# Small edits at the start of a two-attention kernel: two weight loads on another DMA queue, a weight split earlier, a DMA group earlier, another rotation of PSUM banks, another operation in the row maxima

## The chip, the cores and the metric

The kernel runs on one core of one Trainium2 chip. The metric is the device time of one execution in microseconds. A profiled execution additionally leaves a trace: its span runs from the first to the last instruction, and its own time is a little longer than its span.

## The reference

The inputs are float32: 2048 rows of 576, and 32 heads of 18 columns for each of two attentions. Attention A has its own keys and values for every head; attention B shares one key and one value head among its 32 query heads. A gate per row mixes the two results.

```python
def _A_ref(x, wqkv, wo):                       # 32 heads, Dh = 18
    q, k, v = (x @ wqkv) split by head
    p = softmax(q @ k^T * Dh ** -0.5)
    return (p @ v) @ wo
def _B_ref(x, wq, wk, wv, wo):                 # k and v shared by 32 heads
    q = (x @ wq) split by head; k = x @ wk; v = x @ wv
    return (softmax(q @ k^T * Dh ** -0.5) @ v) @ wo
g = sigmoid((x * gate_w).sum(-1, keepdims=True))
return g * _A_ref(...) + (1 - g) * _B_ref(...)
```

## The kernel before

**Numbers as pairs.** Every float32 operand is cut into a high part h (rounded to the type that TensorE multiplies at full rate) and a low part l, the difference. ScalarE or another engine writes h, VectorE or GpSimd writes l = value - h. A projection tile is 14 matmuls: h*h and the two mixed products over the four full rows of 128 of the inner dimension (x dimension 0 to 511), and two matmuls for the last 64, stacked.

**Stage 1, projection of tiles 0 to 2.** All weight columns stand in `wall` as 14 tiles of 128 columns. Tiles 0, 1 and 2 are projected first, for the row chunks c = 0 to 3 of 512 rows each: (tile, chunk) = (0,0), (1,0), (2,0), then the list `FIRST` = (0,1), (1,1), (2,1), (0,2), (0,3), (1,2), (2,2), (1,3), (2,3). Tile 0 holds the shared key, the gate column, the shared value and the first queries of B. x arrives transposed by DMA in two half chunks (`xsh`) and three full ones (`xs`), and `chunk(c)` cuts chunk c: for each half `split_x` has ScalarE write h (`xh`, L388) and VectorE write l (`xl`, L394) and the last 64 rows (L398). `chunk(2)` stands before the result of (1,1) is taken, `chunk(3)` before that of (2,1). `leave` takes a finished projection out of PSUM: ScalarE L284, for tile 0 also L287, VectorE L289. It then stores it to DRAM: tile 0's rows for the first heads by SP's queue (`kq`), everything else by Pool's queue (`qk`). For chunks 1 and 3 of tile 0 it also forms the difference of two key chunks: chunk 1's on GpSimd (L305, L240, L242, stored as `kd`), chunk 3's on VectorE and ScalarE (`ke`). `shared_v` transposes the shared value out of tile 0's results (L326).

**DMA queues.** `dma()` (L163) issues from SP's queue unless told otherwise. An engine's queue is in order: a store that waits for its data holds up everything behind it. SP loads nearly everything and stores `kq`, `kd` and `z_d`. After chunk 0 of tile 0 is stored, SP loads x's last chunk (`load_x(4)`), and then the weights of tiles 3 and 4 (`load_w`, tile `wst`), each as one transfer of 128 rows and two of 64. `first_back` loads the rows back that the next stage needs first (`kdb`, `qs`, `ksb`); `rows_back` loads the others.

**Stage 2, the lead.** The weights of tiles 3 and 4 are projected in half steps (letters A and B: matmuls of 64 rows on two halves of the array, L963), interleaved by a string written out by hand with the row maxima of the first heads. An x in that string is a matmul (L1115) that ScalarE takes out (`xd`, L1119), a y one that VectorE takes with a running maximum (`junk`, `mx`, L1125). GpSimd adds and cuts the results of tiles 3 and 4 (L1101, L240, L242). `prep_w` cuts a weight tile (L250 on ScalarE, L251 on VectorE): tile 3's after the seventh entry of `FIRST`, tile 4's inside the lead. `max_rows` closes the maxima of a head: a reduction, a transpose, and the pair h, l of the result (`mh`, L240 and L242). It runs on VectorE for heads 0 and 1 and with GpSimd for the others.

**Stage 3, the main part.** For each of the 64 heads: scores (L740 maxima, L695 scores), the exponential on ScalarE (L748), the maxima on VectorE (L704), and the products with v accumulated in `acc` (L755). Half steps of the remaining projections are woven in by strings written out by hand.

**Banks.** Seven PSUM banks are handed out. In stage 1 `clk.turn` does it: kind "s" takes banks 0 to 2 in turn, for projections, and kind "m" banks 3 to 6, for the transposes of `shared_v`. From stage 2 on `Clock.first` picks the bank that its own estimate frees first; `turn` leaves behind in what order the banks were given out.

Of the kernel before, what the change touches and what calls it, by code (L numbers as in the profile page):

```python
# [8 lines left out]
F32 = mybir.dt.float32  # L9
F32R = mybir.dt.float32r  # L10
BF16 = mybir.dt.bfloat16
AF = mybir.ActivationFunctionType
OP = mybir.AluOpType
# [15 lines left out]
NT = 5  # L29
FIRST = ((0, 1), (1, 1), (2, 1), (0, 2), (0, 3), (1, 2), (2, 2), (1, 3), (2, 3))  # L30
PRODS = (("h", "h"), ("h", "l"), ("l", "h"))
PROJ = [(a, b, k, 128) for a, b in (("h", "h"), ("l", "h"), ("h", "l")) for k in range(NKT - 1)] + \
# [15 lines left out]
class Clock:  # L48


    def __init__(self):
        self.free = [0.0] * 7
        self.t = self.act = self.dve = self.last = 0.0
        self.mode, self.begun, self.tail = "", [0.0, 0.0], [0.0, 0.0]
        self.turns, self.count, self.held, self.diffs, self.copies = {"s": 0, "m": 0}, 0, {}, [], []
        self.cleared, self.half = 0.0, HALF_MM

    def turn(self, which):
        n = self.turns[which]
        self.turns[which] += 1  # L60
        self.count += 1
        k = n % 3 if which == "s" else 3 + n % 4
        self.free[k] = -1e6 + self.count
        return k

# [91 lines left out]
def gated_mix_kernel(ctx: ExitStack, tc: tile.TileContext, xT, wall, wv, wo, out):  # L157
# [3 lines left out]
    def dma(o, i, eng=None):  # L161
        o, i = (x.bitcast(F32) if x.dtype == F32R else x for x in (o, i))
        return (eng or nc.sync).dma_start(o, i)  # L163
# [46 lines left out]
    def in_turn(which):  # L210
        return bank_tile(clk.turn(which))
# [29 lines left out]
        if l is not None:  # L241
            eng_l.tensor_tensor(l, src, h.bitcast(F32), op=OP.subtract)  # L242

    def load5(t, src, rest=None):
        dma(t[:, 0:4, :], src[0:512, :].rearrange("(p k) m -> p k m", p=P))
        dma(t[0:64, 4, :], src[512:576, :], rest)
        dma(t[64:128, 4, :], src[512:576, :], rest)

# [1 line left out]
        nc.scalar.activation(w["h"], st, AF.Copy)  # L250
        eng_l.tensor_tensor(w["l"], st, w["h"].bitcast(F32), op=OP.subtract)  # L251

    def load_w(mt, rest=None):
        st = wpool.tile([P, NKT, P], F32, name="wst", bufs=5)
        load5(st, wall[mt], rest)
        return st

    def prep_w(st):
        w = {y: wpool.tile([P, NKT, P], F32R, name=f"w{y}", bufs=3) for y in "hl"}
        split_w(st, w, nc.vector)  # L260
        return w
# [4 lines left out]
    def project(mt, c, w, parts=1):  # L266


        fp = in_turn("s")
        g = 512 // parts  # L270
        for i in range(parts):
            products(fp, w, c * 512, g * i, g)
        return leave(mt, c, fp)
# [47 lines left out]
        return c, st  # L321

    def shared_v(c, st):
        pv = in_turn("m")
        for j in range(4):
            nc.tensor.transpose(pv[:, 18 * j:18 * j + 18],  # L326
                                st[ROW_VB:ROW_VB + 18, j * P:(j + 1) * P],
                                ident[ROW_VB:ROW_VB + 18, ROW_VB:ROW_VB + 18])
        nc.vector.tensor_copy(vb[:, 4 * c:4 * c + 4, 0:18],
                              pv[:, 0:72].rearrange("p (j d) -> p j d", d=18))  # L330
# [35 lines left out]
    with tc.tile_pool(name="xs", bufs=1, side="right") as xsp:  # L366
        XS = []

        def load_x(c, rest=None):
            half = c < 2  # L370
            XS.append(xsp.tile([P, NKT, 256 if half else 512], F32, name="xsh" if half else "xs", bufs=2 if half else 3))
            load5(XS[c], xT[:, 256 * c:256 * c + 256] if half else xT[:, 512 * (c - 1):512 * c], rest)

        def main_w(st):

            w = {y: wpool.tile([P, NKT, P], F32R, name=f"w{y}", bufs=3) for y in "hl"}
            nc.scalar.activation(w["h"][:, 0:4], st[:, 0:4], AF.Copy)
            nc.vector.tensor_tensor(w["l"][:, 0:4], st[:, 0:4], w["h"][:, 0:4].bitcast(F32), op=OP.subtract)
            return w

        def last_w(st, w):
            nc.scalar.activation(w["h"][:, 4], st[:, 4], AF.Copy)
            nc.vector.tensor_tensor(w["l"][:, 4], st[:, 4], w["h"][:, 4].bitcast(F32), op=OP.subtract)

        def split_x(c):
            xs = XS[c // 2 + 1][:, :, 256 * (c % 2):256 * (c % 2) + 256] if c > 1 else XS[c]
            cs = slice(c * 256, (c + 1) * 256)
            nc.scalar.activation(X["h"][:, :, cs], xs, AF.Copy)  # L388
            low_x(c, xs)
            last_x(c, xs)  # L390

        def low_x(c, xs):
            cs = slice(c * 256, (c + 1) * 256)
            nc.vector.tensor_tensor(X["l"][:, :, cs], xs[:, 0:4], X["h"][:, 0:4, cs].bitcast(F32), op=OP.subtract)  # L394

        def last_x(c, xs):
            xh = X["h"][64:128, 4, c * 256:(c + 1) * 256]
            nc.vector.tensor_tensor(xh, xs[64:128, 4], xh.bitcast(F32), op=OP.subtract)  # L398

        W = [load_w(0, nc.scalar)]  # L400
        load_x(0, nc.scalar)
        nc.scalar.activation(ones, ones, AF.Copy)
        W.append(load_w(1, nc.gpsimd))
        W.append(load_w(2, nc.gpsimd))
        load_x(1, nc.gpsimd)

        warm = in_turn("m")
        for i in range(6):
            nc.tensor.matmul(warm[:, 0:304], ident, vb.rearrange("p k d -> p (k d)"), start=True, stop=True)
        for c in range(2, 4):  # L410
            load_x(c)
        dma(ones_r.rearrange("a (b c) -> (a b) c", c=32), ones)

        x0, xh = XS[0], X["h"][:, :, 0:256]
        ST = [W.pop(0) for _ in range(3)]
        WP = [main_w(ST[0])]
        nc.scalar.activation(xh[:, 0:2], x0[:, 0:2], AF.Copy)
        nc.vector.tensor_copy(xh[:, 2:4], x0[:, 2:4])
        low_x(0, x0)
        WP.append(main_w(ST[1]))  # L420
        WP.append(main_w(ST[2]))
        last_w(ST[0], WP[0])
        nc.scalar.activation(xh[:, 4], x0[:, 4], AF.Copy)
        last_x(0, x0)
        last_w(ST[1], WP[1])
        last_w(ST[2], WP[2])
        split_x(1)
        FP = [in_turn("s") for _ in range(3)]
        for n in ((0, 12), (12, 14)):
            for mt in range(3):  # L430
                products(FP[mt], WP[mt], 0, 0, 256, *n)
        keep = []

        def chunk(c):
            split_x(2 * c)
            split_x(2 * c + 1)

        for mt in range(3):
            if mt == 2:
                chunk(1)  # L440
                shared_v(*keep.pop())
            products(FP[mt], WP[mt], 0, 256, 256)
            keep.append(leave(mt, 0, FP[mt]))
            keep = [k for k in keep if k]
            if mt == 0:
                load_x(4)
                for m in range(3, NT):
                    W.append(load_w(m))
        for n, (mt, c) in enumerate(FIRST):
            if n == 1:  # L450
                chunk(2)
            if n == 2:
                chunk(3)
            if keep and keep[0][0] <= n - 2:
                shared_v(*keep.pop(0)[1])
            done = project(mt, c, WP[mt], 2 if n == 0 else 1)
            if done:
                keep.append((n, done))
            if (mt, c) == (0, 2):
                first_back()  # L460
            if (mt, c) == (0, 3):
                rows_back()
            if n == 6:
                WP.append(prep_w(W.pop(0)))

    xdp = ph1.enter_context(tc.tile_pool(name="xdp", bufs=1, side="right"))
    small = ctx.enter_context(tc.tile_pool(name="small", bufs=1, side="left"))
# [238 lines left out]
    def max_rows(u, eng=nc.gpsimd):  # L706
# [5 lines left out]
        mt = lead.tile([P, 32], F32, name="mt")  # L712
        nc.vector.transpose(mt, m)  # L713
        mh = lead.tile([P, 2, 32], F32R, name="mh")
        split(mt, mh[:, 0, :], mh[:, 1, :], eng, eng)
        md = m_d[u % 4]
        dma(md, mh.rearrange("p a f -> p (a f)"))
        for b in (SB, MB) if u > NU - 3 else (SB,):
# [368 lines left out]

    def lead_units():
        yield
        for mt in range(3, NT):  # L1090
            w = WP.pop()
            for c in range(4):
                if (mt, c) == (3, 1):
                    for _ in range(NT - 4):
                        WP.append(prep_w(W.pop(0)))
                st = stp.tile([P, 512], F32, name="pst", bufs=3)
                st2 = xdp.tile([P, 512], F32, name="pst2", bufs=2)

                def done(mt=mt, c=c, st=st, st2=st2):
                    hl = stp.tile([P, 2, 512], F32R, name="phl", bufs=4)  # L1100
                    nc.gpsimd.tensor_tensor(st, st, st2, op=OP.add)  # L1101
                    split(st, hl[:, 0, :], hl[:, 1, :], nc.gpsimd, nc.gpsimd)
                    dma(qk_d[:, mt * P:(mt + 1) * P, c * 512:(c + 1) * 512].rearrange("a p f -> p a f"), hl,
                        nc.gpsimd)

                yield Unit([(w[a][:, k, :], X[b][:, k, c * 512:(c + 1) * 512]) for a, b, k, _ in PROJ],
                           512, (st, st2), done, how="both", upper=-1)

    def lead_max(what, low):
        M, h = pairs[what].pop(0)  # L1110
# [187 lines left out]
```

## Time and profile before

| | us |
|---|---|
| median of 3 runs | 2635.0 |
| lowest, highest | 2634.32, 2636.1 |
| profiled execution, its own time | 2633.82 |
| its span | 2632.0 |
| stage 1 in the trace | 0 to 50.5 |
| the lead | 50.5 to about 91 |

In the timeline rows the columns are start, duration, engine, line, operation, written tile and read tiles, shapes and count; a bracket holds the time that the engine had been idle and what ended the idle time. Rows marked SPq, and the DMA rows of POOL, are the issue of a transfer, not the transfer. PEld is the weight load of a matmul; it stands in order ahead of its matmul, so a PEld that waits for a PSUM bank holds TensorE up. The queue table counts packets, MB and the time that their packets took as a share of the 16 DMA engines; q1 is the queue that SP feeds, q0 the one that GpSimd feeds.

### The profile page before, as it was taken

The numbers are of one execution on the slowest core, as the hardware profiler recorded it, in microseconds if no ns is written. First come the engines' busy times: TensorE is split into PE (matmuls) and PEld (weight loads), VectorE is DVE, ScalarE is ACT, GpSimd is POOL, SyncE is SP. The second block draws the span as 40 slices with busy tenths as digits, with TensorE's granted clock in tenths as the row PEclk, the third lists the DMA queues.
The fourth block names the chain that finished last, engine by engine and source line by source line (L and its number), as shares of the span: only waits on it lengthen the run. The fifth ranks groups of instructions, "written<-read, shape, count | busy, mean of one in ns | idle before, by whom it ended". The sixth has DMA issues, their size and how long they took to land.

```text
span 2632.0 us, 66889 instructions
## 1 busy us (share of the span) xinstructions
PE 2621.7 (100%) x25213; PEld 1404.5 (53%) x25213; DVE 2395.4 (91%) x4575; ACT 2447.6 (93%) x4862; POOL 850.5 (32%) x1087
## 2 busy tenths in 40 slices
PE   9999999999999999999999999999999999999999
PEld 7655545545455455554554555545555544545665
DVE  6899999999999999999999999999998999999883
ACT  5999999999999999999999999999999999999887
POOL 3611000211364535644554446443310020012113
PEclk9999999999999999999999999999999999999999
DMA  8412112212343234323544344434432332234312
GB/s 259 140 54 62 36 48 59 75 48 74 96 123 105 91 97 120 113 89 93 152 130 137 119 138 141 142 118 121 141 95 76 101 98 85 61 88 126 110 56 92
DMA packets 176328, 270.28 MB, mean 103 GB/s; under 512 B 58905, under 2 KB 137193, under 8 KB 164625
## 3 DMA queue, kind: packets, MB, share of 16 engines
q1 hardware_dynamic: 159813, 212.70, 28.2%
q0 software_dynamic: 15152, 51.79, 5.3%
q8 instruction: 198, 3.24, 0.5%
q10 hardware_dynamic: 1040, 1.52, 0.2%
q14 instruction: 125, 1.02, 0.1%
HBM read 190.26 MB, written 66.90 MB: 98 GB/s over the span
## 4 chain that ended last, share of the span: by engine, by line
PE 98%; DMA 1%; DVE 0%; ACT 0%; SPq 0%; POOL 0%; issue 0%; ACTq 0%; DVEq 0%
PE acc L755 39%; PE bank L695 29%; PE bank L740 17%; PE bank L963 11%; PE bank L278 1%; PE bank L1115 0%; PE bank L943 0%; DMA xsh<-xT 0%; PE acc L767 0%; DMA R<-r_d 0%; SPq L163 0%; POOL oacc L936 0%; DMA wst<-wall 0%; PE bank L1017 0%; DMA sm<-sum_d 0%
## 5 line engine op out<-in xcount | busy, mean ns | idle before, releaser
L748 ACT ACTIVATE pt<-bank 128x512 f32<-128x512 f32 x4096 | 2146.4, 616 | 120.4 <-PE bank L740 68.7
L704 DVE TENSOR_REDUCE mx<-bank 128x1 f32<-128x512 f32 x3002 | 1886.9, 684 | 118.2 <-PE bank L740 60.3
L740 PE MATMUL bank<-qs,ksb 56*128 56x512 f32 x2688 | 906.8, 424 | 0.0
L695 PE MATMUL bank<-ksb,qs 54*128 54x512 f32 x2270 | 806.4, 426 | 0.0
L755 PE MATMUL acc<-pt,vb 128*19 128x256 f32 (+3 forms) x6144 | 553.2, 455 | 0.0
L695 PEld LDWEIGHTS bank<-ksb,qs 54*128 54x128 f32 x2270 | 382.8, 184 | 318.8 <-ACT pt L748 190.3
L755 PE MATMUL acc<-pt,vg 128*19 128x512 f32 (+3 forms) x5952 | 535.0, 455 | 0.0
L740 PEld LDWEIGHTS bank<-qs,ksb 56*128 56x128 f32 x2688 | 441.1, 184 | 153.9 <-DVE mx L704 63.8
L740 PE MATMUL bank<-qs,ksa 56*128 56x512 f32 x1408 | 466.6, 425 | 0.0
L695 PE MATMUL bank<-ksa,qs 54*128 54x512 f32 x1232 | 439.2, 426 | 0.0
L701 DVE CUSTOM_DVE_ANT_0 junk<-bank,xb 128x512 bf16<-128x512 f32 x500 | 342.9, 686 | 29.4 <-PE bank L740 23.6
L698 ACT ACTIVATE xb<-bank 128x512 f32<-128x512 f32 x500 | 292.6, 606 | 13.7 <-PE bank L740 3.2
L695 PEld LDWEIGHTS bank<-ksa,qs 54*128 54x128 f32 x1232 | 207.8, 184 | 151.1 <-ACT pt L748 87.4
L240 POOL CAST mh<-mt 128x32 fp32r<-128x32 f32 x62 | 13.0, 210 | 831.1 <-DVE mt L713 608.8
L740 PEld LDWEIGHTS bank<-qs,ksa 56*128 56x128 f32 x1408 | 225.5, 184 | 84.2 <-DVE mx L704 31.3
L755 PEld LDWEIGHTS acc<-pt,vb 128*19 128x19 f32 x6144 | 123.1, 97 | 203.1 <-issue 169.6
L755 PEld LDWEIGHTS acc<-pt,vg 128*19 128x19 f32 x5952 | 119.7, 97 | 206.2 <-issue 180.2
L240 POOL CAST rhl<-rst 128x292 fp32r<-128x292 f32 (+2 forms) x81 | 34.0, 420 | 486.7 <-issue 316.4
L963 PE MATMUL bank<-xr,wrh 64*128 64x292 f32 (+1 forms) x1134 | 167.9, 300 | 0.0
L695 PE MATMUL bank<-kdb,qs 54*128 54x512 f32 x372 | 159.8, 430 | 0.0
L963 PEld LDWEIGHTS bank<-xr,wrh 64*128 64x128 f32 x1134 | 139.5, 186 | 2.8
L558 POOL TENSOR_TENSOR xr<-xst,xr 128x876 fp32r<-128x876 f32 (+1 forms) x63 | 130.4, 2070 | 0.0
(171 smaller groups left out, 2397.0 us busy)
## 6 DMA issues: line engine op xcount, KB each, us to landing
qs<-qk SPq DMA_DIRECT2D x366, 144.0 KB
xst<-xT SPq DMA_DIRECT2D x54, 438.0 KB
ksa<-qk SPq DMA_DIRECT2D x132, 144.0 KB
qk<-rhl POOLq DMA_DIRECT2D x54, 292.0 KB, 4.3
ksb<-qk SPq DMA_DIRECT2D x60, 144.0 KB
qk<-phl POOLq DMA_DIRECT2D x16, 512.0 KB, 5.4
onh<-oh POOLq DMA_DIRECT2D x32, 256.0 KB, 3.9
onl<-ol POOLq DMA_DIRECT2D x32, 256.0 KB, 4.7
```

What stands on the lines that cost most here:

```text
L240: eng_h.tensor_copy(h, src)
L278: nc.tensor.matmul(fp[:, p0:p0 + g], w[a][:kr, k, :], X[b][:kr, k, x0 + p0:x0 + p0 + g], start=(n == 0), stop=(n == len(PROJ) - 1))
L558: nc.gpsimd.tensor_tensor(x[:, 5:8, 0:n], t0, x[:, 0:3, 0:n].bitcast(F32), op=OP.subtract)
L695: nc.tensor.matmul(pm, qs[u % 3][b:b + 54, i * P:(i + 1) * P], k, start=True, stop=True)
L698: nc.scalar.activation(MX["x", u, i], pm, AF.Relu)
L701: nc.vector.tensor_tensor_reduce(junk, pm, MX.pop(("x", u, i)), 1.0, -3e38, op0=OP.add, op1=OP.max, accum_out=MX[u][:, i, c:c + 1])
L704: nc.vector.tensor_reduce(MX[u][:, i, c:c + 1], pm, axis=AX.X, op=OP.max)
L740: nc.tensor.matmul(ps, kst(u)[b:b + 56, i * P:(i + 1) * P], qs[u % 3][b:b + 56, c * 512:(c + 1) * 512], start=True, stop=True)
L748: nc.scalar.activation(pt, ps, AF.Exp, scale=SCALE)
L755: nc.tensor.matmul(acc[32 * j:32 * j + 19, a:b], v_of(u, i), PT[u, i, j][:, a:b], start=(i == 0), stop=(i == 15), skip_group_check=True)
L963: nc.tensor.matmul(u.fp[op][:, 0:u.n], x[b:b + 64], y[b:b + 64], start=(n == 0), stop=(n == last))
```

## The change

The change has five parts.

1. `load_w` and `load5` get an argument `main`, and both transfers' queues become GpSimd's for tiles 3 and 4; the loop stands where it stood, after chunk 0 of tile 0 was stored.
2. `prep_w` is called after the seventh and after the eighth entry of `FIRST`, so tile 4 is cut there and not in the lead.
3. `first_back` is called after (2,1), one entry of `FIRST` earlier than before.
4. Projections and `shared_v` of stage 1 draw from one rotation "g" of all seven banks; the warm-up matmuls keep "m".
5. Where `max_rows` runs on VectorE, h is written by `tensor_tensor` with the maximum of a value and itself, not by a CAST.

```diff
-        k = n % 3 if which == "s" else 3 + n % 4
+        k = n % 3 if which == "s" else 3 + n % 4 if which == "m" else n % 7
...
-    def load5(t, src, rest=None):
-        dma(t[:, 0:4, :], src[0:512, :].rearrange("(p k) m -> p k m", p=P))
+    def load5(t, src, rest=None, main=None):
+        dma(t[:, 0:4, :], src[0:512, :].rearrange("(p k) m -> p k m", p=P), main)
...
     def project(mt, c, w, parts=1):
-        fp = in_turn("s")
+        fp = in_turn("g")
...
     def shared_v(c, st):
-        pv = in_turn("m")
+        pv = in_turn("g")
...
-        FP = [in_turn("s") for _ in range(3)]
+        FP = [in_turn("g") for _ in range(3)]
...
             if mt == 0:
                 load_x(4)
                 for m in range(3, NT):
-                    W.append(load_w(m))
+                    W.append(load_w(m, nc.gpsimd, nc.gpsimd))
...
-            if (mt, c) == (0, 2):
+            if (mt, c) == (2, 1):
                 first_back()
             if (mt, c) == (0, 3):
                 rows_back()
-            if n == 6:
+            if n in (6, 7):
                 WP.append(prep_w(W.pop(0)))
+        while keep:
+            shared_v(*keep.pop(0)[1])
...
-        split(mt, mh[:, 0, :], mh[:, 1, :], eng, eng)
+        if eng is nc.vector:
+            eng.tensor_tensor(mh[:, 0, :], mt, mt, op=OP.max)
+            eng.tensor_tensor(mh[:, 1, :], mt, mh[:, 0, :].bitcast(F32), op=OP.subtract)
+        else:
+            split(mt, mh[:, 0, :], mh[:, 1, :], eng, eng)
...
     def lead_units():
-                if (mt, c) == (3, 1):
-                    for _ in range(NT - 4):
-                        WP.append(prep_w(W.pop(0)))
```

TensorE's instructions keep their order from the first to the last; only the banks that they name differ. What moves on the other engines is shown in three pieces.

SP's queue in stage 1, as a piece of the difference: `xs` is x's last chunk, `kq`, `kd` and `z_d` are the stores of tile 0, `kdb`, `qs` and `ksb` the loads of `first_back`.

```order
 L163 DMA xs<-xT 64x512 x2
-L163 DMA wst<-wall 128x512
-L163 DMA wst<-wall 64x128 x2
-L163 DMA wst<-wall 128x512
-L163 DMA wst<-wall 64x128 x2
 L163 DMA kq<-phl 54x2x512
```

The six weight transfers (rows with x2 are two) leave the place between x's last chunk and the stores of (0,1).

GpSimd's queue at the same place of the program, as a piece of the difference: `qk<-phl 24x2x512` is the store of (0,0), the two of 128x2x512 are those of (1,0) and (2,0).

```order
 L163 DMA xsh<-xT 64x256 x2
 L163 DMA qk<-phl 24x2x512
+L163 DMA wst<-wall 128x512
+L163 DMA wst<-wall 64x128 x2
+L163 DMA wst<-wall 128x512
+L163 DMA wst<-wall 64x128 x2
 L163 DMA qk<-phl 128x2x512 x2
```

They now stand behind the store of (0,0) and ahead of the stores of (1,0) and (2,0).

ScalarE's end of stage 1 and start of the lead, before: `phl` rows take (2,2), (1,3) and (2,3) out of PSUM, `wh` rows cut a weight tile, `xd` and `pst` rows belong to the lead.

```order
L284 ACTIVATE phl<-bank_525 128x512
L250 ACTIVATE wh<-wst 128x640
L284 ACTIVATE phl<-bank_548 128x512
L284 ACTIVATE phl<-bank_567 128x512
L1119 ACTIVATE xd<-bank_630 128x512
L1119 ACTIVATE xd<-bank_638 128x512
L1119 ACTIVATE xd<-bank_648 128x512
L1119 ACTIVATE xd<-bank_660 128x512
L1119 ACTIVATE xd<-bank_670 128x512
L973 ACTIVATE pst<-bank_617 128x512
L250 ACTIVATE wh<-wst 128x640
```

And with the change:

```order
L284 ACTIVATE phl<-bank_525 128x512
L250 ACTIVATE wh<-wst 128x640
L284 ACTIVATE phl<-bank_548 128x512
L250 ACTIVATE wh<-wst 128x640
L284 ACTIVATE phl<-bank_571 128x512
L1120 ACTIVATE xd<-bank_634 128x512
```

Tile 4's cut goes from behind the first `pst` of the lead to between (1,3) and (2,3); VectorE's L251 moves with it.

More of the change, by code (lines that the diff above doesn't have):

```diff
@@ L54, in __init__ @@
         self.mode, self.begun, self.tail = "", [0.0, 0.0], [0.0, 0.0]
-        self.turns, self.count, self.held, self.diffs, self.copies = {"s": 0, "m": 0}, 0, {}, [], []
+        self.turns, self.count, self.held, self.diffs, self.copies = {"s": 0, "m": 0, "g": 0}, 0, {}, [], []
         self.cleared, self.half = 0.0, HALF_MM
@@ L251, in split_w, with load_w @@
         eng_l.tensor_tensor(w["l"], st, w["h"].bitcast(F32), op=OP.subtract)
-    def load_w(mt, rest=None):
+    def load_w(mt, rest=None, main=None):
         st = wpool.tile([P, NKT, P], F32, name="wst", bufs=5)
-        load5(st, wall[mt], rest)
+        load5(st, wall[mt], rest, main)
         return st
@@ L443, in gated_mix_kernel @@
             keep.append(leave(mt, 0, FP[mt]))
-            keep = [k for k in keep if k]
             if mt == 0:
@@ L447, in gated_mix_kernel @@
                 for m in range(3, NT):
-                    W.append(load_w(m))
+                    W.append(load_w(m, nc.gpsimd, nc.gpsimd))
+            keep = [k for k in keep if k]
         for n, (mt, c) in enumerate(FIRST):
@@ L1089, in lead_units, with done @@
         yield
-        for mt in range(3, NT):
-            w = WP.pop()
-            for c in range(4):
-                if (mt, c) == (3, 1):
-                    for _ in range(NT - 4):
-                        WP.append(prep_w(W.pop(0)))
[L1096 to L1107, printed above, removed]
+        for mt, c in [(mt, c) for mt in range(3, NT) for c in range(4)]:
+            w = WP[mt]
+            st = stp.tile([P, 512], F32, name="pst", bufs=3)
+            st2 = xdp.tile([P, 512], F32, name="pst2", bufs=2)
+            def done(mt=mt, c=c, st=st, st2=st2):
+                hl = stp.tile([P, 2, 512], F32R, name="phl", bufs=4)
+                nc.gpsimd.tensor_tensor(st, st, st2, op=OP.add)
+                split(st, hl[:, 0, :], hl[:, 1, :], nc.gpsimd, nc.gpsimd)
+                dma(qk_d[:, mt * P:(mt + 1) * P, c * 512:(c + 1) * 512].rearrange("a p f -> p a f"), hl, nc.gpsimd)
+            yield Unit([(w[a][:, k, :], X[b][:, k, c * 512:(c + 1) * 512]) for a, b, k, _ in PROJ],
+                       512, (st, st2), done, how="both", upper=-1)
     def lead_max(what, low):
```

## The prediction

> **What bounds the kernel now.** I read the page first: shares of busy time and the chain that ended last.
>
> ```profile
> PE 2621.7 (100%) x25213; PEld 1404.5 (53%) x25213; DVE 2395.4 (91%) x4575; ACT 2447.6 (93%) x4862; POOL 850.5 (32%) x1087
> PE 98%; DMA 1%; DVE 0%; ACT 0%; SPq 0%; POOL 0%; issue 0%; ACTq 0%; DVEq 0%
> ```
>
> TensorE carries the chain for 98% of the span. Since its instructions keep their order, the change can move the end only through moments in which TensorE stands still. Next the windows by stage (PE busy comes first after the window's length).
>
> ```profile
> 0.00:50.50 50.50, 48.28 (x252) 39.32 (x252) 29.76 (x44) 22.51 (x34) 16.43 (x26) 1.00 0.84 261
> 50.50:91.00 40.50, 38.97 (x309) 31.60 (x309) 33.98 (x98) 34.50 (x67) 28.44 (x37) 1.00 0.66 196
> 91.00:2632.00 2541.00, 2534.49 (x24654) 1333.56 (x24653) 2331.64 (x4434) 2390.59 (x4762) 805.62 (x1025) 1.00 0.33 98
> ```
>
> TensorE is idle for 50.50 - 48.28 = 2.2 us in stage 1 and 40.50 - 38.97 = 1.5 us in the lead. That caps what the edits can give at about 4 us; 0.2% of this kernel is 5.3 us, about what a measurement of it can tell from no change. The DMA engines are 84% busy in stage 1, so what a transfer is moved next to matters there.
>
> The timelines of TensorE and ScalarE then show what stage 1 hangs on: the first matmuls of (0,3), and x's last chunk.
>
> ```profile
> 33.27 1.16 PE L278 MATMUL bank<-xh,wh 128*128 128x512 f32 x4
> 30.74 2.44 ACT L388 ACTIVATE xh<-xs 128x1280 fp32r<-128x1280 f32 x2 [3.52 <-DMA xs<-xT]
> ```
>
> ScalarE sat idle for 3.52 us until x's last chunk landed at 30.74, and finished cutting at 30.74 + 2.44 = 33.18. TensorE began (0,3) at 33.27 with no idle time in its row. So the slack is 0.09 us: from there on, each us that x's last chunk lands later is a us of TensorE.
>
> **Part 1, weights by GpSimd's queue.** How large they are, when SP issued them, and when GpSimd's queue issued its stores:
>
> ```profile
> wst<-wall SPq DMA_DIRECT2D x5, 256.0 KB
> wst<-wall SPq DMA_DIRECT2D x4, 32.0 KB
> 20.87 2.28 SPq L163 DMA_DIRECT2D xs<-xT  x3
> 23.19 6.81 SPq L163 DMA_DIRECT2D wst<-wall  x6
> 17.95 0.64 POOL L163 DMA_DIRECT2D qk<-phl  x1 [13.13 <-DVE phl L289]
> 19.15 0.76 POOL L163 DMA_DIRECT2D qk<-phl  x1 [0.56 <-DVE phl L289]
> 24.00 0.73 POOL L163 DMA_DIRECT2D qk<-phl  x1 [4.09 <-DVE phl L289]
> ```
>
> Tiles 3 and 4 are 2 x 256 + 4 x 32 = 640 KB, 0.655 MB. Before, SP issued them behind x's last chunk, in its own queue. Now GpSimd issues them from 18.6 on: by the 0.64 us of the row at 17.95, six issues take 3.8 us, until about 22.4. They come before x's last chunk has landed, and from another queue. The store of (1,0) slips from 19.15 to about 22.4; that of (2,0), at 24.00, need not slip, and TensorE reads neither in this stage.
>
> What two queues do to each other is in the queue table, for 24 to 28 and for 28 to 31 us:
>
> ```profile
> DMA packets 613, 1.19 MB, mean 297 GB/s; under 512 B 40, under 2 KB 40, under 8 KB 613
> q1 hardware_dynamic: 605, 1.16, 96.9%
> q0 software_dynamic: 8, 0.03, 2.4%
> DMA packets 580, 1.03 MB, mean 344 GB/s; under 512 B 99, under 2 KB 249, under 8 KB 580
> q1 hardware_dynamic: 413, 0.48, 49.0%
> q0 software_dynamic: 167, 0.55, 47.2%
> ```
>
> In 28 to 31 us the two queues split the engines evenly (49.0 and 47.2%), at nearly the same total rate. If the weights share like that, all 0.655 MB pass before x's last chunk is complete: 0.655 MB at 344 and at 297 GB/s are 1.9 and 2.2 us. I take 2.0 us, 1.9 after the slack. The lower bound is nothing: in 24 to 28 us the store issued at 24.00 moved hardly anything (2.4%) while x's chunk took the engines; were the weights to wait like that, x would lose nothing. I see no gain here, because the group before (0,3) ends at 33.27 however early x lands. The upper bound is that the store of (2,0) also passes first: another 512 KB, 0.524 MB, 1.5 to 1.8 us; then 2.2 + 1.8 - 0.09 gives at most 3.9 us. I take the even split because the late store had only just been issued, while the weights' issues lie 1.6 to 5.4 us earlier. [...]
>
> **Part 2, tile 4's cut.** Where it stood, and where TensorE then stood still (the PEld rows are what held it):
>
> ```profile
> 55.77 0.75 ACT L250 ACTIVATE wh<-wst 128x640 fp32r<-128x640 f32 x1
> 56.55 0.83 DVE L251 TENSOR_TENSOR wl<-wst,wh 128x640 fp32r<-128x640 f32 x1 [0.60 <-ACT wh L250]
> 57.05 0.18 PEld L1115 LDWEIGHTS bank<-kdb,qs 54*128 54x128 f32 x1 [0.43 <-ACT xd L1119]
> 58.04 0.18 PEld L1115 LDWEIGHTS bank<-ksb,qs 54*128 54x128 f32 x1 [0.80 <-DVE mx L1125]
> 57.06 0.49 PE L1115 MATMUL bank<-kdb,qs 54*128 54x512 f32 x1
> 58.04 0.49 PE L1115 MATMUL bank<-ksb,qs 54*128 54x512 f32 x1 [0.49 <-DVE mx L1125]
> ```
>
> The cut takes ScalarE 0.75 and VectorE 0.83 us, plus 0.60 us in which VectorE waits for ScalarE, just when both hand banks back. TensorE's loads wait 0.43 and 0.80 us for those banks, 1.23 together. The least it costs is the 0.49 us in the matmul's own bracket. I take 1.0 us of gain, nearer the loads' rows, since these name what came late. At its new place the cut is free: ahead of the take-out of (2,3), ScalarE and VectorE idle.
>
> ```profile
> 50.63 0.60 ACT L284 ACTIVATE phl<-bank 128x512 fp32r<-128x512 f32 x1 [2.52 <-PE bank L278]
> 51.26 0.69 DVE L289 TENSOR_TENSOR phl<-bank,phl 128x512 fp32r<-128x512 f32 x1 [2.43 <-ACT phl L284]
> ```
>
> 2.5 and 2.4 us of idle time cover 0.75 and 0.83. Without that cover, the lead's first banks would come back that much later.
>
> **Part 5, the maxima.** The stall it aims at, what GpSimd did then, and the nearest rows for a two-input operation of VectorE beside GpSimd:
>
> ```profile
> L240 DVE CAST mh<-mt x2: 292/650/1007, 79.6 to 114.0; 128x32 fp32r<-128x32 f32 x2
> L242 DVE TENSOR_TENSOR mh<-mt,mh x2: 191/192/194, 80.6 to 114.3; 128x32 fp32r<-128x32 f32 x2
> 79.24 1.29 POOL L242 TENSOR_TENSOR phl<-pst,phl 128x512 fp32r<-128x512 f32 x1
> 81.47 0.49 PE L1115 MATMUL bank<-ksb,qs 54*128 54x512 f32 x1 [1.04 <-DVE mx L1125]
> 26.07 1.91 POOL L305 TENSOR_TENSOR pd<-pst 18x512 f32<-18x512 f32 x1
> 26.86 1.40 DVE L398 TENSOR_TENSOR xh<-xs,xh 64x256 fp32r<-64x256 f32 x1
> 33.30 0.42 DVE L398 TENSOR_TENSOR xh<-xs,xh 64x256 fp32r<-64x256 f32 x1
> ```
>
> At 79.6 the CAST took 1.007 us and ended with GpSimd's subtraction (79.24 + 1.29 = 80.53); TensorE then idled 1.04 us. A TENSOR_TENSOR of that size takes 0.19 us, so the swap is worth up to 0.82 us if it escapes GpSimd. But L398, a TENSOR_TENSOR whose inputs both lie in SBUF, took 0.42 us alone and 1.40 beside GpSimd's L305, ending at 28.26, just after GpSimd's 27.98. The maximum reads the same tile twice, also in SBUF. I take 0, and keep 0.82 as the other end. [...] The second call, at 114.0, has no more than 0.1 us to give.
>
> **Parts 3 and 4.** SP's queue and the first use of what `first_back` loads:
>
> ```profile
> 28.81 2.15 POOL L242 TENSOR_TENSOR pdhl<-pd,pdhl 18x512 fp32r<-18x512 f32 x1
> 40.68 0.57 SPq L163 DMA_DIRECT2D kdb<-kd  x1
> 52.03 0.39 PE L1115 MATMUL bank<-kdb,qs 54*128 54x512 f32 x1
> qk<-phl POOLq DMA_DIRECT2D x9, 512.0 KB, 5.7
> ```
>
> `kdb` was issued at 40.68 and used at 52.03 with no wait, so issuing it earlier gains nothing. SP will now wait there for the key difference, ready at 28.81 + 2.15 = 30.96, to be stored and landed: 5.7 us by the store landings that the trace shows, so until about 37. Queued behind it are the stores of (0,2), whose data I expect at about the same time, and then `rows_back`; without the six weight issues (6.81 us) SP is ahead. Cost 0. The seven banks gain nothing either: the first matmul of (0,3) reuses a bank of an earlier group, and its row shows no wait. They cover one thing: ScalarE's take-outs behind the late cut of x come about 2 us later and could hold three banks; seven leave room.
>
> **The sum.** +1.9 (x's last chunk) - 1.0 (cut) + 0 + 0 = +0.9 us. On the profiled execution that is a span of 2632.0 + 0.9 = 2632.9; its own time, 2633.82, lies 1.2 us under the median of the runs shown, 2635.0. From the median: 2635.9 us.
>
> **The rivals.**
> - A, the forecast, chance 0.52. If a third of the weights passes before x's last chunk starts, the hold is 2/3 of 2.0 less the slack, 1.2 us; if a third of the (2,0) store goes along, 1.9 + 0.6 = 2.5 us. With the cut at 1.23 and 0.49 A spans 2635.0 to 2637.0.
> - B, the weights take nothing from x, as the 2.4% row has it: -1.0, so 2634.0; chance 0.17. The even split of 28 to 31 us speaks against it.
> - C, the maximum doesn't wait for GpSimd: +0.9 - 0.8 = +0.1, so 2635.1; chance 0.10. Part 5 as meant; L398 speaks against it.
> - D, all that GpSimd's queue holds passes before x: 3.9 - 1.0 = +2.9, so 2637.9; chance 0.11. It decides if the store of (2,0) starts before x has landed; at 24.00 it came too late for that.
> - E, the main part settles differently, on the side of slower by over 0.2%. It hands its 2541 us over between engines that are 91 to 100% busy, and its weight loads wait for ScalarE all along:
>
> ```profile
> L695 PEld LDWEIGHTS bank<-ksb,qs 54*128 54x128 f32 x2270 | 382.8, 184 | 318.8 <-ACT pt L748 190.3
> ```
>
> These 190.3 us lie under running matmuls. If a start in another phase brought 3% of them, 5.7 us, to the surface, 2635.9 would become 2641.6; from 2.3% on it decides the class. Against it: orders and strings of the main part are unchanged, and only bank numbers and a start shifted by a us differ. Chance 0.06, and 0.04 for the same on the other side.
>
> **The numbers.** A to D make 0.90 within 0.2%; the rest is 0.04 faster and 0.06 slower. The range takes in B with the cut at 1.23 and the maximum free (-2.05, 2632.9) and D with the cut at 0.49 (+3.4, 2638.4), rounded outwards: 2632.5 to 2638.5.
>
> **What would show it.** Right: TensorE idle 1.2 to 2.5 us just ahead of (0,3), with ScalarE's cut of x's last chunk starting near 32.7 and not at 30.74; no L250 in the lead, and no wait of a load near the place of 57 us; the new TENSOR_TENSOR of head 0 as long as the CAST was, if GpSimd's subtraction still runs. Wrong: (0,3) starting at 33.3 (B); the new TENSOR_TENSOR at 0.2 us while GpSimd subtracts (C); a main part longer or shorter than 2541 us by more than 1 us (E).

## The result, and the profile after

| | before | after |
|---|---|---|
| median, us | 2634.97 (21 runs) | 2638.52 (21 runs) |
| lowest, highest | 2633.44, 2636.76 | 2636.27, 2644.28 |
| profiled execution: own time, span | 2633.82, 2632.0 | 2637.38, 2635.6 |

The ratio is 1.0015, 95% interval 1.001 to 1.0021: 3.55 us, or 0.13%, slower. That is within 0.2%, but 0.02 us above the forecast's range (2632.5 to 2638.5), and 2.6 us above its 2635.9. After's executions lie much further apart than before's: 8.0 us against 3.3.

ScalarE's and TensorE's timeline rows around (0,3), after:

```profile
33.02 2.43 ACT L388 ACTIVATE xh<-xs 128x1280 fp32r<-128x1280 f32 x2 [5.75 <-DMA xs<-xT]
35.51 1.19 PE L278 MATMUL bank<-xh,wh 128*128 128x512 f32 x4 [2.04 <-ACT xh L388]
38.13 1.91 PE L278 MATMUL bank<-xl,wh 128*128 128x512 f32 x4
```

ScalarE cuts x's last chunk from 33.02 on instead of 30.74. TensorE idles 2.04 us and starts (0,3) at 35.51 instead of 33.27: +2.24. Four matmuls then take 1.91 us. Before, the same four took:

```profile
35.17 1.09 PE L278 MATMUL bank<-xl,wh 128*128 128x512 f32 x4
```

The reason is in the windows of after, two stretches side by side (length; busy PE, PEld, DVE, ACT, POOL; granted clock; DMA share and GB/s):

```profile
33.24:36.65 3.41, 1.36 (x6) 0.97 (x6) 2.26 (x3) 3.41 (x5) 0.00 (x0) 1.00 0.57 208
36.65:40.07 3.42, 3.42 (x10) 2.64 (x9) 2.56 (x5) 0.27 (x1) 1.07 (x2) 0.50 0.77 211
```

TensorE is idle for 2.05 of the 3.41 us before 36.65, and for the next 3.42 us its granted clock is 0.50. That costs about 1.6 us: TensorE's starts, compared one by one with before's, are 2.24 us late at the start of (0,3) and 3.85 at its end.

In the lead, TensorE's load rows of after (all that wait 0.2 us or more from 50 to 80 us) and the rows of head 0's maximum:

```profile
54.35 0.76 PEld L969 LDWEIGHTS bank<-xh,wh 64*128 64x128 f32 x8 [0.35 <-issue]
58.61 0.19 PEld L969 LDWEIGHTS bank<-xh,wh 64*128 64x128 f32 x2 [0.22 <-DVE mx L1126]
59.22 0.18 PEld L1116 LDWEIGHTS bank<-ksb,qs 54*128 54x128 f32 x1 [0.24 <-DVE mx L1126]
81.80 1.29 POOL L242 TENSOR_TENSOR phl<-pst,phl 128x512 fp32r<-128x512 f32 x1
82.11 1.02 DVE L718 TENSOR_TENSOR mh<-mt 128x32 fp32r<-128x32 f32 x1
84.04 0.49 PE L1116 MATMUL bank<-ksb,qs 54*128 54x512 f32 x1 [1.06 <-DVE mx L1126]
```

The lead starts 3.83 us late (50.52, 54.35). The waits of 0.43 and 0.80 us are gone, and at head 0's closing the lag is 84.04 - 81.47 = 2.57: the cut gave 1.26. The new maximum takes 1.02 us beside GpSimd's subtraction, as the CAST did, and TensorE idles 1.06 us as before. TensorE's last matmul stands in the two timelines at, before and after:

```profile
2626.11 0.29 PE L943 MATMUL bank<-wol,qs 128*128 128x288 f32 x1
2629.53 0.29 PE L949 MATMUL bank<-wol,qs 128*128 128x288 f32 x1
```

That is a lag of 3.42, so 0.85 us come on top between head 0 and the end, 0.36 of them between 2601 and 2605 us. The profile tells +2.24 (late x), +1.6 (half clock), -1.26 (cut) and +0.85 (the rest), 3.4 in all. What it doesn't tell is why seven of the 21 executions took 2641 to 2644.

### The profile page after: what moved, and what is told of

It reads as the page before. It is cut to its first block, busy times and chain, and to the rows that moved or that the text cites. A ratio compares the mean times of both kernels' runs of the same rounds, so it can differ in the third digit from the quotient of the medians.

```text
span 2635.6 us, 66893 instructions
## 1 busy us (share of the span) xinstructions
PE 2622.6 (100%) x25213; PEld 1405.1 (53%) x25213; DVE 2395.9 (91%) x4575; ACT 2447.0 (93%) x4862; POOL 855.1 (32%) x1093
## 3 DMA queue, kind: packets, MB, share of 16 engines
q14 instruction: 125, 1.02, 0.1%
## 4 chain that ended last, share of the span: by engine, by line
PE 98%; DMA 1%; ACT 0%; DVE 0%; issue 0%; POOL 0%; SPq 0%; ACTq 0%; DVEq 0%
PE acc L761 39%; PE bank L697 29%; PE bank L746 17%; PE bank L969 11%; PE bank L278 1%; PE acc L773 1%; PE bank L949 0%; DMA xs<-xT 0%; PE bank L1116 0%; DMA xsh<-xT 0%; ACT xh L388 0%; POOL oacc L942 0%; DMA wst<-wall 0%; PE bank L1023 0%; DVE rl L1013 0%
## 5 line engine op out<-in xcount | busy, mean ns | idle before, releaser
L703 DVE CUSTOM_DVE_ANT_0 junk<-bank,xb 128x512 bf16<-128x512 f32 x500 | 342.6, 685 | 30.4 <-PE bank L746 24.2
```

The costliest lines, as they stand in the source:

```text
L703: nc.vector.tensor_tensor_reduce(junk, pm, MX.pop(("x", u, i)), 1.0, -3e38, op0=OP.add, op1=OP.max, accum_out=MX[u][:, i, c:c + 1])
```

## The experiments

Each pair in square brackets is the 95% interval of the ratio to the kernel before, whose median on the chips of these runs lay between 2635.1 and 2635.8. Where the text says "by the starts", TensorE's matmuls were compared one by one, in order, with those of the profile of before.

**Part 1 undone.**

```diff
-                    W.append(load_w(m, nc.gpsimd, nc.gpsimd))
+                    W.append(load_w(m))
```

> The change with its weight loads of tiles 3 and 4 back on SP's queue, all else as changed. Theory S (the loads share the DMA engines with x's last chunk, TensorE idles for it, and its clock then falls to half): x lands near 30.7 and not 33.0 us, no idle time ahead of (0,3), no half clock there, and the gain of the cut, 1.2 us, is left: 2633.7 us, 1.3 us under before. Rival R1 (the earlier first_back or the seven banks make x's cut late): (0,3) still starts near 35.5 and the time stays at 2638 us. Rival R2 (a half clock that comes by itself): x lands at 30.7, but a window of half clock remains, about 2635.4 us.

Measured: 2635.45 (2633.26 to 2638.16), [0.9989, 1.0006]. Around (0,3) it came as the theory has it: ScalarE's cut starts at 29.51, TensorE doesn't idle. But the expected 2633.7 wasn't reached. The timelines of GpSimd, VectorE and TensorE near 115 us show a wait that neither profile of before and after has:

```profile
112.68 2.04 POOL L242 TENSOR_TENSOR vwl<-wvs,vwh 128x864 fp32r<-128x864 f32 x1
112.71 2.06 DVE L718 TENSOR_TENSOR mh<-mt 128x32 fp32r<-128x32 f32 x1
116.03 0.73 PE L746 MATMUL bank<-qs,ksb 56*128 56x512 f32 x2 [1.42 <-DVE mx L706]
```

This is the second call of the maximum, head 1's. VectorE's operation falls against a 2.04-us subtraction of GpSimd (a cut of value weights), lasts as long, and TensorE waits 1.42 us; by the starts it falls back by 2.06 us there. In before and after's profiles VectorE came while GpSimd was in the cast just ahead of that subtraction, and got through (after):

```profile
115.99 0.91 POOL L240 CAST vwh<-wvs 128x864 fp32r<-128x864 f32 x1
116.54 0.40 DVE L718 TENSOR_TENSOR mh<-mt 128x32 fp32r<-128x32 f32 x1
```

**Part 1 alone**: the kernel before, with the argument `main` and the diff's call of `load_w`.

> The kernel before with the first part alone: the weight loads of tiles 3 and 4 by GpSimd's queue. Theory S: x lands near 33.0 us, TensorE idles 2.0 us ahead of (0,3), one or two windows of half clock follow (1.7 us each), and nothing is gained in the lead: 2635.0 + 2.2 + 1.7 to 3.4 = 2638.9 to 2640.6 us. Rival R1 (other parts make it late): 2635.0 us. Rival R2: x late, but no half clock in (0,3), 2637.2 us.

Measured: 2640.21 (2637.66 to 2642.16), [1.0005, 1.0023]. The hold is the largest seen, and yet the clock stays at 1.00 in the window before (0,3) and in the one after it:

```profile
36.36 1.19 PE L278 MATMUL bank<-xh,wh 128*128 128x512 f32 x4 [3.29 <-ACT xh L388]
31.23:34.64 3.41, 1.84 (x9) 1.18 (x7) 0.38 (x1) 0.76 (x1) 0.75 (x1) 1.00 0.73 281
34.64:38.05 3.41, 1.69 (x7) 1.42 (x8) 2.81 (x3) 3.12 (x5) 0.00 (x0) 1.00 0.16 63
```

The same wait of 1.42 us for head 1's maximum is there, this time behind a CAST of 2.05 us. So the time lies where the theory put it (2638.9 to 2640.6), but for another reason: by the starts this profile has 3.1 us from the late x and 2.0 from head 1's wait, and no half clock.

**No long idle time ahead of (0,3)**: after, with nine matmuls that nobody reads.

```diff
+            if n == 4:
+                fill = in_turn("g")
+                for _ in range(9):
+                    nc.tensor.matmul(fill, WP[0]["h"][:, 0, :], X["h"][:, 0, 0:512], start=True, stop=True)
```

> The change with nine more matmuls of 512 columns just ahead of (0,3), about 2.05 us of TensorE's time, into a bank that nobody reads: TensorE works while it would wait for x. Theory S (idle time is what lowers the clock): (0,3) starts where it did, near 35.5, but takes 3.3 and not 5.1 us, the granted clock stays at 1.00, and 1.7 to 3.4 us of 2638.5 go: 2636.0 us, with less scatter between executions. Rival R2 (the clock falls whatever TensorE does): (0,3) takes 5 us again, 2638.5 us or more.

Measured: 2636.93 (2635.88 to 2637.74), [0.9992, 1.0009], though x's chunk came later still (34.45):

```profile
36.93 1.19 PE L278 MATMUL bank<-xh,wh 128*128 128x512 f32 x4 [1.21 <-ACT xh L388]
```

1.21 us of idle time are left, no half clock follows in this profile, and (0,3) takes 3.3 us again. With matmuls added and x no earlier, the median is 1.6 us below after's, or 2.4 if each is taken against before on its own chip. That fits the half clock's price, though head 1's meeting, a wait of 0.24 us in this profile and 0.9 by the starts, may differ as well.

**Half the weights**: tile 3's on GpSimd's queue, tile 4's on SP's.

```diff
+                    W.append(load_w(m, nc.gpsimd, nc.gpsimd) if m == 3 else load_w(m))
```

> The change with only tile 3's weights on GpSimd's queue; tile 4's are on SP's behind x's last chunk as before. Theory S, sharing by bytes: x is late by half of 2.28 us, 1.1 us, so it lands at 31.9 and (0,3) starts 1.1 us late. If an idle of 1 us leaves the clock alone: 2635.0 + 1.1 - 1.2 = 2634.9 us; if a half window follows, 2636.5 us. Rival R3 (not the bytes but the later store of (1,0), or having a second queue at work at all, makes x late): late by 2 us as with both, 2637 us or more, or not late at all, 2633.7 us.

Measured: 2636.27 (2634.58 to 2638.64), [0.9991, 1.0008].

```profile
31.02 2.44 ACT L388 ACTIVATE xh<-xs 128x1280 fp32r<-128x1280 f32 x2 [3.85 <-DMA xs<-xT]
```

With both tiles on GpSimd's queue ahead of x's landing, ScalarE's cut starts at 33.0 to 34.5 in the four profiles that have it; with none, at 29.5 to 31.2 in eight. Half of them, at 31.0, can't be told from none; against both it saves 2 us or more, so the delay doesn't come from the first bytes on a second queue. But the theory's 31.9, half the delay for half the bytes, didn't come either. What the weights push back counts too: GpSimd's store of (1,0), 512 KB, was issued at 19.15 in before and took 5.7 us to land, until 24.9, before most of x's bytes moved. With one tile ahead of it (20.15) it took 5.7 us as well; with two (21.84, in after) it took 8.6 us, until 30.4, beside x. Whether the weights' own bytes or this store makes x late, no run separates.

**The same queue, later**: the weights are issued by GpSimd behind the key difference.

```diff
             if n == 1:
                 chunk(2)
+                for m in range(3, NT):
+                    W.append(load_w(m, nc.gpsimd, nc.gpsimd))
```

> The change with the weight loads on GpSimd's queue as changed, but issued behind GpSimd's difference of the keys (ahead of the store of (1,1), near 31 us), when x's last chunk has landed. Theory S (what costs is that they move while x's last chunk moves): x lands near 30 us, no idle time ahead of (0,3), clock at 1.00, the same time as with the weights on SP's queue, 2635.4 us. Rival R4 (GpSimd's queue is the wrong one for weights, whenever): 2637 us or more.

Measured: 2635.49 (2633.66 to 2636.22), [0.9989, 1.0006].

```profile
30.45 3.26 POOL L163 DMA_DIRECT2D wst<-wall  x6
29.47 2.44 ACT L388 ACTIVATE xh<-xs 128x1280 fp32r<-128x1280 f32 x2 [2.73 <-DMA xs<-xT]
113.34:116.75 3.41, 1.98 (x22) 0.84 (x15) 3.38 (x5) 2.06 (x5) 3.33 (x3) 1.00 0.04 10
116.75:120.16 3.41, 3.41 (x24) 1.33 (x25) 1.72 (x4) 1.44 (x3) 2.73 (x5) 0.50 0.16 41
```

Issued from 30.45 on, the weights take nothing from x, and the store of (1,0) stands ahead of them again: what costs is the moment, not the queue. But head 1's wait of 1.4 us is followed here by a stretch of half clock.

**The new maximum alone** (part 5 of the diff on the kernel before).

> The kernel before with the fifth part alone: h of the maxima of heads 0 and 1 by a TENSOR_TENSOR and not by a CAST. Theory P (both kinds wait for GpSimd): head 0's TENSOR_TENSOR takes 1.0 us as the CAST did, TensorE idles 1.0 us near 81 us, the time stays at the kernel before's 2635.8 us. Rival C (only the CAST waits): 0.2 us instead of 1.0, 2635.0 us.

Measured: 2635.82 (2634.94 to 2638.32), [0.9992, 1.001]. The answer on the tile `mh` (count; shortest, mean and longest ns; starts in us; shapes):

```profile
L716 DVE TENSOR_TENSOR mh<-mt x2: 1024/1236/1449, 79.8 to 114.2; 128x32 fp32r<-128x32 f32 x2
```

1.02 us for head 0, as the CAST had; 1.45 for head 1, where it met GpSimd.

**Maxima closed by GpSimd.** First heads 0 and 1 (on top of part 1 undone), then head 1 alone, again on top of part 1 undone:

```diff
-            max_rows((T + LEAD) // 16 - 1, nc.gpsimd if T > 16 else nc.vector)
+            max_rows((T + LEAD) // 16 - 1)
```

> The change with its weight loads back on SP's queue and the maxima of heads 0 and 1 closed with GpSimd, as for the other heads, and not on VectorE. Theory P (VectorE's two-input instructions stand behind a running GpSimd instruction, 1.0 us for head 0 and, depending on which comes first, 0 to 2 us for head 1): VectorE is no longer held, the idle 1.04 us of TensorE near 80 us and the 1.42 us that the first experiment shows at 116 us go. The pair of head 0 is ready up to 1.3 us later, which can cost up to 1 us at the first scores. 2635.45 - 0.4 to 2.4 = 2633.0 to 2635.0 us, less scatter. Rival Q (these waits don't come from GpSimd): 2635.4 us, with both waits still there.

Measured: 2634.36 (2632.01 to 2635.87), [0.9985, 1.0003]. TensorE's wait near 80 us is gone, but head 0's pair is ready and stored later, and the first score waits 2.10 us for it, where at most 1 was expected:

```profile
88.73 0.47 PE L746 MATMUL bank<-qs,ksb 56*128 56x512 f32 x1 [2.10 <-DMA qs<-m_d]
```

> As the run before it, but only head 1's maxima with GpSimd; head 0's stay on VectorE. Theory P: the wait near 80 us stays (1.04 us), that at 116 us never comes: 2635.45 - 0 to 1.4 = 2634.0 to 2635.4 us and less scatter than the first experiment. Rival Q: the wait at 116 us appears again in some executions, 2635.4 us.

Measured: 2633.4 (2631.8 to 2634.1), [0.9981, 0.9998]: below before and after, and below the 2634.0 to 2635.4 expected. With head 1 off VectorE, nothing waits near 115 us. But something new stands in the lead. Its first load, ScalarE's take-out of (2,3), a wait of TensorE, and head 0's closing:

```profile
51.02 0.76 PEld L969 LDWEIGHTS bank<-xh,wh 64*128 64x128 f32 x8 [0.35 <-issue]
52.05 0.60 ACT L284 ACTIVATE phl<-bank 128x512 fp32r<-128x512 f32 x1 [2.32 <-DMA qk<-phl]
55.58 0.49 PE L1116 MATMUL bank<-kdb,qs 54*128 54x512 f32 x1 [0.55 <-DVE mx L1126]
81.64 0.50 PE L1116 MATMUL bank<-ksb,qs 54*128 54x512 f32 x1 [1.07 <-DVE mx L1126]
```

From its first load to head 0's closing the lead takes 30.62 us here. That is only 0.33 less than before's 30.95 (50.52 to 81.47), though the cut is moved; after took 29.69. The run with parts 3 and 4 alone, below, shows where the rest went.

**The same edit on after and on before, and parts 3 and 4 alone.**

> The changed kernel with head 1's maxima closed by GpSimd, so that VectorE's wait for GpSimd near 115 us can't occur. Beside the kernel with the same head 1 and the weights on SP's queue (2633.4) it differs in part 1 alone. Theory (part 1 costs the late x chunk, 2.2 to 2.3 us, and the half clock after TensorE's idle time, 1.6): 2636.4 to 2637.4, with the cut of x's last chunk starting near 33.0 and an idle time of about 2 us ahead of (0,3); its runs above 2640 should stay if they come from the clock. Rival (much of the 3.5 us between the two kernels comes from the meeting at head 1): 2634.5 to 2635.7, and no run above 2640.

Measured: 2635.7 (2634.16 to 2637.53), [0.9995, 1.0013]. This is the upper edge of the rival's range, and no run comes near 2640. The hold is there in full, without a half clock in this profile; the last two rows are the lead's first load and head 0's closing, 29.69 us apart:

```profile
36.60 1.21 PE L278 MATMUL bank<-xh,wh 128*128 128x512 f32 x4 [2.64 <-ACT xh L388]
31.63:35.04 3.41, 2.34 (x11) 1.60 (x9) 0.84 (x2) 0.92 (x1) 0.75 (x1) 1.00 0.68 260
35.04:38.45 3.41, 1.85 (x8) 1.46 (x9) 2.93 (x4) 2.97 (x5) 0.00 (x0) 1.00 0.43 145
53.94 0.76 PEld L969 LDWEIGHTS bank<-xh,wh 64*128 64x128 f32 x8 [0.35 <-issue]
83.63 0.50 PE L1116 MATMUL bank<-ksb,qs 54*128 54x512 f32 x1 [1.07 <-DVE mx L1126]
```

> The kernel before with head 1's maxima closed by GpSimd; nothing else. Beside the changed kernel with the weights on SP's queue and the same head 1 (2633.4) it lacks the cut's move, parts 3 and 4 and head 0's maximum. Theory (the cut's move keeps its 1.15 to 1.26 us to the end once head 1's meeting is out of the way): 2634.5 to 2634.7, so 0.3 to 0.9 under the kernel before, and a scatter of 2 to 3 us where the kernel before has 5. Rival (the cut's gain is lost again before the end, and 2633.4 came from head 1 alone): 2633.4.

Measured: 2633.92 (2633.43 to 2635.16), [0.9989, 1.0007]: 1.2 us below the before of the same chip, with 1.7 us between its 11 runs where before has 3.8 between 27. It lies between the theory's 2634.5 and the rival's 2633.4, and the medians leave 0.5 us for the cut; interval widths of 2 us and more don't separate that from 1.2. Its profile has the lead's two waits (0.45 and 0.80 us) that the cut's move removes.

> The kernel before with parts 3 and 4 alone: first_back one entry sooner, and stage 1's banks from one rotation of seven. Theory (both cost nothing): within 0.5 us of the kernel before, 2634.5 to 2636.0, TensorE's starts in stage 1 and in the lead the same to 0.1 us. Rival (the wait for the key difference in SP's queue holds up the stores and loads behind it, or seven banks move the take-outs): a start of the lead later by 0.3 us or more, or a wait of a score for qs, ksb or kdb at 52 to 90 us.

Measured: 2636.49 (2635.08 to 2637.95), [0.9998, 1.0015], above the 2636.0 that the theory allowed, with no difference shown by the interval. In its profile:

```profile
54.70 0.18 PEld L1115 LDWEIGHTS bank<-kdb,qs 54*128 54x128 f32 x1 [0.47 <-DVE mx L1125]
114.69 2.00 DVE L240 CAST mh<-mt 128x32 fp32r<-128x32 f32 x1
119.33:122.74 3.41, 3.41 (x26) 1.39 (x27) 2.04 (x5) 1.65 (x4) 2.10 (x3) 0.50 0.31 85
```

A load of the lead waits 0.47 us and leaves TensorE 0.3 us later; the rest of its span is head 1's meeting and a half clock behind it, 3.5 us by the starts, which this kernel shares with others. Neither of the rival's signs is there: the lead starts 0.14 us late, and no score waits for its rows. But a take-out moved, as the rival had it, the one of (2,3):

```profile
51.16 0.60 ACT L284 ACTIVATE phl<-bank 128x512 fp32r<-128x512 f32 x1 [2.85 <-DMA qk<-phl]
```

In before it starts 0.11 us after the lead's first load, released by TensorE's bank. Here it starts 0.50 us after it (50.66), released by a store: that of (2,2), issued at 46.10 and 5.0 us on its way. VectorE's half, GpSimd's next store and its clearing of `mx`, and VectorE's first running maximum follow in a row, and TensorE's load waits for that maximum's bank. This release by a store is in all six profiles with parts 3 and 4 and x on time. It isn't in the three with these parts and a late x, nor in the four without them. Which of the two parts does it, no run separates.

## Why the prediction was right or wrong

Since head 1 can be taken out of the way, the difference splits into four comparisons of medians:

| from | to | us |
|---|---|---|
| part 1 undone, head 1 on GpSimd: 2633.4 | after, head 1 on GpSimd: 2635.7 | part 1: +2.3 |
| before, head 1 on GpSimd: 2633.92 | part 1 undone, head 1 on GpSimd: 2633.4 | parts 2 to 5: -0.5 |
| before, head 1 on GpSimd: 2633.92 | before: 2635.14 | head 1 in before: +1.2 |
| after, head 1 on GpSimd: 2635.7 | after: 2638.52 | head 1 in after: +2.8 |

2.3 - 0.5 + 2.8 - 1.2 = 3.4. This adds up by construction, to 2638.52 - 2635.14, so it proves nothing; the single rows are what the table tells. The kernels ran on different chips, whose medians of before differ by up to 0.5 us here, and no single row is sharper than about 2 us by its interval; the runs of the first row's two kernels just don't overlap (up to 2634.1, and from 2634.16).

The first two rows hide an exchange. Where x is late, the lead starts 2.9 us later (53.94 against 51.02) but takes 0.9 less (29.69 against 30.62), because the store that parts 3 and 4 made the last take-out wait for has landed by then. So part 1 costs more than +2.3 ahead of the lead, and parts 2 to 5 give less than the cut alone would.

- **x's last chunk, +1.9 forecast: right in kind, somewhat small.** The profile of after has +2.24 with 2.04 us of idle time; in two others with part 1, (0,3) starts 3.1 and 3.3 us later than before's 33.27. The runs with the weights back on SP and with the same issues later show that it comes from what GpSimd's queue moves while x is under way. It wasn't the weights alone that shared: the last of them, issued at 21.33, landed after 6.5 us, at 27.8, and behind them moved the stores. The forecast had seen that the store of (1,0) slips, but priced it at nothing, since TensorE doesn't read it. In after, GpSimd's queue took 68.5% and SP's 27.8% in 28 to 31 us:

```profile
q0 software_dynamic: 250, 0.84, 68.5%
q1 hardware_dynamic: 184, 0.32, 27.8%
```

  The forecast took the even split of time from 28 to 31 us of before (49.0 and 47.2%). In these rows the time isn't split evenly: GpSimd's queue moved 0.84 MB in 250 packets, 3.4 KB each, and SP's 0.32 MB in 184, 1.7 KB each.
- **What follows the idle time, not in the sum: the first step that failed.** By the forecast, "each us that x's last chunk lands later is a us of TensorE", and no more. In after's profile the idle time cost 1.6 more, through the granted clock. The run with filler matmuls, 1.6 us lower, agrees; that with head 1 on GpSimd shows that the half clock needn't come. How many of after's executions have it isn't known.
- **The cut, -1.0 forecast: right for after.** The lead is 1.26 us shorter in the profile of after, a little over the upper bound of 1.23. With x on time the late take-out takes part of it back: 1.10 are left with part 1 undone, 0.72 with the weights issued later, 0.40 with half of them, and 0.33 with part 1 undone and head 1 on GpSimd. That fits the 0.5 that the medians show. The cut wasn't tried alone.
- **The maximum of head 0, 0 forecast: right.** 1.02 us in after, 1.02 alone, against a CAST's 1.01. C falls.
- **"The second call has no more than 0.1 us to give": the second step that failed.** It was true of one execution, where the CAST of 0.29 us happened to come ahead of GpSimd's subtraction. In seven of the nine profiles with head 1 on VectorE it met it. There TensorE's row waits 0.2 to 1.4 us, and by the starts 0.9 to 2.1 us are lost, 3.5 in the two where a half clock follows. Over many executions, by the medians, it costs before 1.2 us, and after 2.8. Why after meets it more dearly isn't shown: its late start shifts the meeting, but neither of the two profiles, before's and after's, has one. By these medians it is the larger part of what was missing: 1.6 of 2638.5 - 2635.9 = 2.6 us.
- **Parts 3 and 4, 0 forecast: right for after, for a reason that the sum doesn't have.** By themselves they make the last take-out of stage 1 wait for a store, which costs 0.3 us in the lead of their profile, and 0.2 to 0.9 in four profiles where the cut is moved as well; the intervals don't show it. In after x is so late that the store has landed.
- **Rivals.** A's hold, 1.2 to 2.5 us, came in after's profile, but what followed it isn't in A. B falls: (0,3) did start late. D's time is close to the result, and its condition was met in after's profile: the store of (2,0), issued at 24.05, landed after 8.3 us, at 32.4, just ahead of x's cut at 33.02. But the hold was 2.24 us, not 3.9. E falls in this profile: the 0.85 us behind head 0 are under its 1 us and far from its 5.7. Where head 1 meets GpSimd the main part is longer than that, but not by the wait for ScalarE that E is made of.

Open: after's 2641 to 2644 seem to need head 1 on VectorE, since none of 11 runs without it passes 2637.6. That they hold two half clocks fits their mean granted clock of 0.998, against 0.999 or 1.0 in the others. It also fits an estimate: the profiled 2637.4, which had the one half clock in (0,3) and no meeting, and 3.5 us for a meeting with a half clock behind it make 2640.9, and six of the seven lie between 2641.0 and 2641.6. But no profile caught one.

## What to carry to other kernels

A transfer moved to another queue can still be in the way of what it used to stand behind, and so can what it pushes back in its new queue: here x's cut started at 33.02 instead of 30.74. Move it in time, not only in queue; the same issues later gave 2635.49 instead of 2638.52. A gain of one edit can be taken back by another: measure the stretch that it aims at, here the lead, in every run. A short VectorE operation on the path that may fall beside GpSimd must be priced by GpSimd's longest instruction in its neighbourhood (here 2.06 us beside a subtraction of 2.04), not by what one profile shows (0.29); moving it to GpSimd, where its result isn't due soon, gave the best version here, 2633.4 against 2635.5 of before on the same chip. And idle time of TensorE can cost nearly as much again through the clock: in after 1.6 us on top of 2.04, though no half clock came with the 2.64 of after with head 1 on GpSimd.

## What the hardware showed that was not expected

- **The clock.** Half-clock stretches inside a run lasted 3.41 us in all three profiles that have one: in (0,3) in after (36.65 to 40.07), behind head 1 in the run with the weights issued later (116.75 to 120.16) and in that with parts 3 and 4 (119.33 to 122.74). The changes of the clock lie on a raster of that length in after: it is full for 30.72 us, half for 3.413 and full for 2594.13, which are 9, 1 and 760 times 3.413. Stretches of the other runs are laid on the same raster here, counted from each run's first full clock. 2.05 us without a matmul in the stretch of 3.41 before was enough in after. In the run with part 1 alone 1.57 and 1.72 us in two such stretches in a row were not; there 3.29 us of idle time was split between them. Behind head 1 even 1.43 us (1.98 busy, matmuls of 56 rows) were enough in the run with the weights issued later, and 1.37 (2.04 busy) in that with parts 3 and 4, while 1.42 (2.00 busy) with part 1 undone were not:

```profile
115.92:119.33 3.41, 2.04 (x23) 0.89 (x15) 3.28 (x6) 2.11 (x5) 3.33 (x5) 1.00 0.04 10
112.94:116.36 3.42, 2.00 (x21) 0.82 (x20) 3.38 (x4) 2.34 (x5) 3.34 (x3) 1.00 0.03 6
```

  In before and after, from the first full clock to the stretch with the last matmul, a half clock followed the stretch with 1.33 us of matmuls at the end of before and the one with 1.36 in after, and none of the others, of which the lowest has 2.09. Of the six stretches of other runs shown here with 1.69 to 2.04 it followed two, with 1.98 and 2.04, and not those with 1.69 and 1.84 (part 1 alone), 1.85 (after with head 1 on GpSimd) and 2.00. So busy time alone does not decide there, and these runs don't settle what does. It also mattered how a wait fell on the raster: the 3.29 us of part 1 alone, split over two stretches, cost no clock, and the 2.04 us of after, within one, did.
- **The meeting of VectorE and GpSimd** made head 1's operation several times as long, a CAST as much as a TENSOR_TENSOR: the CAST took 0.29 us in before and 2.05 with part 1 alone, the TENSOR_TENSOR 0.40 us in after and 2.06 with part 1 undone. Whether they meet differs between kernels and, to judge by the scatter, between executions. Moving head 1 to GpSimd narrowed that from 3.8 us (27 runs) to 1.7 (11) for before, and from 8.0 (21) to 3.4 (11) for after.
